# Moving the row maxima of attention to the steps with products with v, and two start times in the layer behind it

## The chip, the cores and the metric

The kernel is one program on one core of a Trainium2 chip. A core has a matrix engine (PE, with its weight loads shown apart as PEld), a vector engine (DVE), a scalar engine (ACT), GpSimd (POOL), and SyncE (SP), whose queue issues most DMAs. Each engine works through its own instructions in the order in which they were written, and waits on semaphores where it needs what another engine makes. The metric is the device time of one execution in microseconds; the median of the runs is compared.

## The reference

The work is attention over 32 heads (4 batches of 8) with pooled queries, then a dense layer with a gate, then a mixture of experts. The part that the change touches is the first, and the start of the second:

```python
q_pool = q.reshape(B, H, S // 2, 2, D).mean(axis=3)
scores = scale * np.matmul(q_pool, k.transpose(0, 1, 3, 2))
scores = scores - np.max(scores, axis=-1, keepdims=True)
attn = np.exp(scores)
attn = attn / (np.sum(attn, axis=-1, keepdims=True) + 1e-09)
x = np.matmul(attn, v)                      # 576 queries, 1152 keys, 64 columns a head
...
h = x @ w_in                                # 2304 tokens, 512 -> 2048
x = (h * (1.0 / (1.0 + np.exp(-1.702 * h)))) @ w_out
```

## The kernel before

**Attention** works on 16 pairs of heads, one after the other; a pair's two heads stand on partitions 0 to 63 and 64 to 127. A pair is 14 steps, one for each entry of UNITS: steps 0 to 8 take 320 queries against one block of 128 keys, steps 9 to 12 take the other 256 queries against two blocks, step 13 against the last one. The loop counter `g` runs over all steps of all pairs, and `p, i = divmod(g, NU)` with NU = 14.

At each step `score_unit` has PE compute the scores (tile `ss`, eight or sixteen matmuls in pairs, one of a pair for each head): products of the high and low parts of q and k, and one product of ONE with M, which subtracts the row's maximum. ACT then takes the exponential (tile `E`). Two steps behind, `av_group` multiplies groups of E by v (tile `av`), always at steps 4, 7, 10, 13 and 1 (AV_AT). GpSimd adds E up for the row sums (`acc`, `ds`), except for the first three blocks, which DVE reduces (`r`, at steps 4 and 10). `den` turns the sums into `dn` on PE at step 10 of the next pair.

**The maxima** come ahead of the scores, since M must be there at a pair's step 0. `max_unit(p, i)` is one of 14 units for a pair: units 0 to 11 are two matmuls (tile `xs`, 384 keys, one for each head), unit 12 is two and unit 13 one with a block-diagonal operand `BD` that holds the last queries of both heads. Behind each matmul DVE reduces the tile to a maximum (L233). The tiles come from a pool of three PSUM buffers, which the transposed maxima (`mt`) use too. Behind unit 13 `max_rows` reduces to `m9`, and two steps later `max_rows_put` has PE transpose it (`mt`), DVE split it in `mh` and `ml`, and SP bring both to M by eight small DMAs. Before the change each step has one unit, LEAD = 19 steps ahead of the score step with the same number, so a pair's last unit stands at step 8 of the pair before it.

The order within a step is: score, unit, rows, products with v, den, what the agenda `ag` holds for this step (r, mt, pieces of the weights' conversion, x), GpSimd's sums, then BESIDE, which prepares coming pairs (loads, `q_high`, `k_high`, at step 7 `q_low` on DVE and `k_low` on GpSimd). Agenda entries for the weights and x stand at steps 13 and 1.

**The dense layer** (`ffn`) goes through chunks of tokens, the first of 768 in two pieces. A step is twelve matmuls of layer 1 into `h` (two PSUM buffers), a gate on ACT and DVE, and two steps later nine matmuls of layer 2 into `acc`. In the first chunk the weights still arrive as 8-byte floats, and each of 28 blocks is converted by seven DVE instructions (L453 to L459) and three on ACT (L461 to L463). `blocks` is a generator that gives them one by one, and `fill(n)` writes the next n of them into the queues: three and then three or four at each step of the first chunk. ACT's share is written by `act` at the following step. For the next chunk `xload` brings a tile of x and the reciprocals of its row sums into `xraw`, of which there is one buffer; `xnorm` multiplies them, for chunk 1 on DVE; `xsplit` makes high and low parts.

Of the kernel before, what the change touches and what calls it, by code (L numbers as in the profile page):

```python
# [39 lines left out]
def pieces(n):  # L40
    k = -(-n // 384)
    return [(i * (n // k), n // k) for i in range(k)]
# [6 lines left out]
NU = len(UNITS)  # L49
EARLY = 2  # L50
AV_AT = (4, 7, 10, 13, 1)
GROUPS = [range(0, 3), range(3, 6), range(6, 9), range(9, 12), range(12, 14)]


# [17 lines left out]
class Kernel:  # L72
# [54 lines left out]
    def attention(self, ctx):  # L127
# [11 lines left out]
        N = NPAIR  # L139
# [23 lines left out]
        ag = Agenda()  # L163
# [71 lines left out]
        def max_rows(p):  # L235

            m9 = sm.tile([P, 9], F32, name="m9", tag="m9")
            V.reduce_max(m9, st[p]["mx"], axis=AX.X)
            max_rows_put(0, m9) if p == 0 else ag.at(ag.now + 2, max_rows_put, p, m9)
# [90 lines left out]
            for u in range(2):  # L330
                eng.dma_start(self.DEN[hp * 2 + u:hp * 2 + u + 1, b * Q:b * Q + Q], dr[64 * u:64 * u + 1])

        LEAD = 19

        BESIDE = [(0, v_load, 1), (2, q_high, 2), (3, k_high, 2, 0), (4, k_high, 2, 1), (5, k_high, 2, 2),
                  (7, q_low, 1), (7, k_low, 1), (8, loads, 3), (13, q_add, 3)]
# [21 lines left out]
        for u in range(2):  # L358
            g = NU * 1 + 3 + u * (NU * 3 + 6)
            calm = [x for x in range(g + 7, g + 5 * NU) if x % NU in AV_AT[3:]]  # L360
            ag.at(g, self.wload, u)
            ag.at(g + 6, weights, u, [g + 6, *calm[:6], calm[4] + 1, calm[5] + 1, calm[6]])

        for u in range(2, 2 * EARLY):
            g = NU * (N - 1) - 5 + 8 * (u - 2)
# [3 lines left out]
            ag.at(NU * N - 8 + 5 * n, self.wload, 2 * EARLY + n)  # L369
        for b in range(8):  # L370
            ag.at(NU * (8 + b) + AV_AT[3] - 10, operands, b % 4, b // 4)
        for g in range(-LEAD, NU * N + 20):
            p, i = divmod(g, NU)
            ag.now = g
            if 0 <= p < N:
                score_unit(p, i)
            px, ix = divmod(g + LEAD, NU)
            if 0 <= px < N:
                max_unit(px, ix)
                if ix == NU - 1:  # L380
                    max_rows(px)
            pa, ia = divmod(g - 2, NU)
            for j, r in enumerate(GROUPS):
                if 0 <= pa < N and ia == r[-1]:
                    av_group(pa, j)
            if i == 10 and 0 < p <= N:
                den(p - 1)
            ag.run(g)
            if 0 <= p < N:
                sum_unit(p, i)  # L390
            for f, *of in start.get(g + LEAD, ()):
                f(*of)
            for step, f, ahead, *of in BESIDE:
                if step == i and 0 <= p and p + ahead < N:
                    f(p + ahead, *of)
            if g == -LEAD + 12:
                empty_lists()
            if i == 12 and 1 <= p < N and p % 4 == 0:
                self.recip(sm, p // 4 - 1, ag, 9)
            if g == NU * N:  # L400
                nc.scalar.activation(warm[:, 1:2], warm[:, 0:1], AF.Sigmoid)
# [89 lines left out]
    def ffn(self, ctx):  # L491
# [34 lines left out]
        ag = Agenda()  # L526
# [38 lines left out]
        def fill(k):  # L565
            for _ in range(k):
                f = fq.pop(0) if fq else next(splits, None)
                if f:
                    f()
# [181 lines left out]
                fq.append(fin)  # L751

        constants()
        steps = [(c, fb, pc) for c in range(len(CH)) for fb in range(NF) for pc in range(len(pieces(CH[c])))]
        first = {(c, fb): g for g, (c, fb, pc) in reversed(list(enumerate(steps)))}
        LAG = 2
        for g in range(len(steps) + LAG):
            ag.now = g
            if g < len(steps):
                c, fb, pc = steps[g]  # L760
                fa, fb_ = (2, 3) if CH[c] >= 384 else (1, 2)
                if g == 2:
                    self.recip(sm, B - 1, ag, 3)
                if c == 0:
                    fa, fb_ = 3, 3 + pc
                layer1(c, fb, pc, fa, fb_)
                if fb == 0 and pc == 0 and c + 1 < len(CH):
                    for j in range(ND):
                        for q in range(len(pieces(CH[c + 1]))):
                            g0 = first[0, 12] + 2 * j - 1 if c == 0 else first[c, 4] + 2 * j  # L770
                            ag.at(g0, xload, c + 1, j, q)
                            ag.at(g0 + 1, xnorm, c + 1, j, q)
                            ag.at(first[c, NF - 1] if c == 0 else g0 + 4, xsplit, c + 1, j, q)
            if g >= LAG:
                c2, f2, p2 = steps[g - LAG]
                layer2(c2, f2, p2)
                if f2 == NF - 1:
                    if c2 == 0 and p2 == 0:
                        while splits.gi_frame:
                            fill(1)  # L780
                            act()
                        rctx.close()
                        late["o"] = self.pool(ctx, "m_o", 2)
                        late["wg"] = late["o"].tile([P, 9, DM], F32, name="wg", tag="wg", bufs=1)
                        dma(late["wg"][:, 0:8], self.wgT.partition_broadcast(P))
                        dma(late["wg"][:, 8], self.w_skip.partition_broadcast(P))
                        for d in range(ND):
                            dma(wgd[:, d, 0:8], self.wgT[:, d * P:d * P + P].rearrange("e p -> p e"))
                            dma(wgd[:, d, 8:9], self.w_skip[d * P:d * P + P].rearrange("(p a) -> p a", a=1))
                    o, n = pieces(CH[c2])[p2]  # L790
                    grp = tuple((C0[c2] + o) // P + i for i in range(n // P))
                    if c2 < len(CH) - 1:
                        todo.extend((grp, i) for i in range(len(grp)))
            if g < len(steps) + LAG - 1:
                rstep()
                ag.run(g)
            if not (self.first or todo or fq or live[0]) and self.listed == NT - CH[-1] // P:

                self.first = late["o"].tile([P, 9, DM], F32, name="first", tag="wg", bufs=1)
                for m in range(4):  # L800
                    self.first_expert_load(m)
                for m in range(8):
                    ag.at(max(g + 2 + m // 2, first[len(CH) - 1, m] + LAG + 1), self.first_expert_split, m)

                ps = hp.tile([P, 8], F32, name="cn", tag="h")
                nc.tensor.matmul(ps, ONE, mac[self.listed], start=True, stop=True)
                V.tensor_scalar(self.early, ps[:, 0:1], P - 0.5, float(P), op0=ALU.is_gt, op1=ALU.mult)
                dma(self.ids_e, self.LIST[0:P])
                V.memset(self.x_e, 0.0)
                nc.gpsimd.indirect_dma_start(  # L810
                    out=self.x_e, out_offset=None, in_=self.X2[0:C0[-1]],
                    in_offset=bass.IndirectOffsetOnAxis(ap=self.ids_e[:, 0:1].bitcast(U32), axis=0),
                    bounds_check=C0[-1] - 1, oob_is_err=False,
                )
# [270 lines left out]
```

## Time and profile before

| | |
|---|---|
| median of 3 runs | 1052.24 us (1047.6 to 1054.67) |
| the profiled execution, its own time | 1049.92 us |
| its span | 1048.1 us |
| PE busy | 996.8 us, 95% |
| DVE busy | 768.9 us, 73% |
| ACT busy | 501.9 us, 48% |
| POOL busy | 454.2 us, 43% |
| mean granted clock of TensorE | 0.984 |

The span is from the first to the last instruction; 1.8 us of the execution lie around it. Matmuls are pipelined, so PE counts as busy while the next matmul is held back by less than the last one's tail; what a group of matmuls costs is read from the start of its first to the start of what follows it. A timeline row gives the start, the length of the merged instructions, engine, line, operation, the tiles written and read, the shapes and the count, and in brackets the idle time before it with what ended it.

### The profile page before, as it was taken

How to read it: one execution, taken by the hardware profiler on the slowest of the kernel's cores; microseconds unless marked ns; L12 is line 12 of the kernel's file. 1: busy time of each engine (PE TensorE's matmuls, PEld its weight loads, DVE VectorE, ACT ScalarE, POOL GpSimd, SP SyncE). 2: the span in 40 equal slices, each digit the busy share in tenths (PEclk: the TensorE clock that was granted, in tenths of full speed). 3: DMA queues.
4: the chain of work that ended last, by engine and by line, in shares of the span. 5: the costliest groups of instructions: out<-in, count | busy, mean ns of one | idle time of the engine just before them, and what ended most of it. 6: DMA issues, size and time to landing. Idle time of an engine off the chain costs nothing. (4 is left out here: it accounts for less than half of the span.)

```text
span 1048.1 us, 18986 instructions
## 1 busy us (share of the span) xinstructions
PE 996.8 (95%) x7002; PEld 787.3 (75%) x7002; DVE 768.9 (73%) x1643; ACT 501.9 (48%) x928; POOL 454.2 (43%) x306
## 2 busy tenths in 40 slices
PE   6999999999999999999997999999999997998994
PEld 4766667666766676698886888888889885876773
DVE  7767777778877778799977689787575564656824
ACT  2555555555555554655644422332333261555723
POOL 3798999999999998500000001101111003223212
PEclk9999999999999999999999999999999998998998
DMA  4232232223333322333342520212211234738501
GB/s 166 67 101 81 81 101 82 81 81 97 97 96 96 97 72 71 99 102 122 123 132 81 173 71 16 71 33 60 71 48 44 81 115 145 266 105 285 164 21 51
DMA packets 64321, 103.34 MB, mean 99 GB/s; under 512 B 18630, under 2 KB 34630, under 8 KB 64072
## 3 DMA queue, kind: packets, MB, share of 16 engines
q1 hardware_dynamic: 60068, 96.34, 28.6%
q0 software_dynamic: 3904, 5.15, 1.6%
q8 instruction: 67, 1.10, 0.4%
q14 instruction: 54, 0.44, 0.1%
q10 hardware_dynamic: 228, 0.30, 0.1%
HBM read 90.04 MB, written 17.35 MB: 102 GB/s over the span
## 5 line engine op out<-in xcount | busy, mean ns | idle before, releaser
L233 DVE TENSOR_REDUCE mx<-xs 128x1 f32<-128x384 f32 x432 | 212.7, 550 | 75.5 <-PE xs L230 70.1
L274 ACT ACTIVATE E<-ss 128x640 f32<-128x640 f32 (+1 forms) x224 | 174.0, 787 | 149.0 <-PE ss L273 120.7
L290 POOL TENSOR_TENSOR acc<-acc,E 128x640 f32<-128x640 f32 (+1 forms) x94 | 179.4, 1909 | 16.4 <-ACT E L274 12.3
L310 PE MATMUL av<-E,v 128*64 128x256 f32 (+1 forms) x1152 | 157.1, 413 | 0.0
L599 PE MATMUL h<-xh,wih 128*128 128x384 f32 (+1 forms) x448 | 141.3, 315 | 9.9 <-ACT wih L463 7.7
L599 PE MATMUL h<-xh,wil 128*128 128x384 f32 (+1 forms) x448 | 140.0, 312 | 0.6 <-DVE wil L459 0.5
L599 PE MATMUL h<-xl,wih 128*128 128x384 f32 (+1 forms) x448 | 139.9, 312 | 0.1
L476 POOL TENSOR_TENSOR xa<-xraw 128x256 f32<-128x256 f32 (+1 forms) x16 | 15.5, 970 | 261.3 <-DMA xraw<-RD 256.1
L310 PEld LDWEIGHTS av<-E,v 128*64 128x64 f32 x1152 | 75.6, 136 | 56.0 <-issue 15.0
L626 PE MATMUL acc<-woh,gl 128*128 128x512 f32 x288 | 114.8, 399 | 0.0
L624 PE MATMUL acc<-woh,gh 128*128 128x512 f32 x288 | 114.8, 399 | 0.0
L625 PE MATMUL acc<-wol,gh 128*128 128x512 f32 x288 | 114.5, 398 | 0.0
L230 PE MATMUL xs<-kh,qh 64*128 64x384 f32 x384 | 101.9, 388 | 7.9 <-ACT kh L210 7.2
L273 PE MATMUL ss<-qh,kh 64*128 64x320 f32 (+1 forms) x576 | 107.3, 339 | 2.0 <-ACT E L274 2.0
L604 ACT ACTIVATE g<-h 128x384 f32<-128x384 f32 (+1 forms) x112 | 49.4, 441 | 116.1 <-PE h L599 116.0
L606 ACT ACTIVATE gh<-g 128x384 fp32r<-128x384 f32 (+1 forms) x112 | 53.8, 480 | 104.6 <-DVE g L605 104.6
L599 PEld LDWEIGHTS h<-xh,wih 128*128 128x128 f32 x448 | 84.2, 188 | 18.5 <-ACT wih L463 11.0
L643 DVE CUSTOM_DVE_ANT_0 junk<-xs,wg 128x512 bf16<-128x512 f32 x135 | 95.5, 707 | 2.0
L605 DVE TENSOR_TENSOR g<-h,g 128x384 f32<-128x384 f32 (+1 forms) x112 | 55.7, 497 | 55.9 <-ACT g L604 54.5
L273 PE MATMUL ss<-M,ONE 64*128 64x320 f32 (+1 forms) x576 | 94.2, 294 | 0.7 <-DMA M<-ml 0.6
L273 PE MATMUL ss<-qh,kl 64*128 64x320 f32 (+1 forms) x576 | 92.2, 293 | 0.0
L273 PE MATMUL ss<-ql,kh 64*128 64x320 f32 (+1 forms) x576 | 92.1, 293 | 0.0
(195 smaller groups left out, 2069.6 us busy)
## 6 DMA issues: line engine op xcount, KB each, us to landing
stage<-w SPq DMA_DIRECT2D x40, 512.0 KB
qd<-qT SPq DMA_DIRECT2D x16, 576.0 KB
v<-v SPq DMA_DIRECT2D x16, 576.0 KB
kr<-kT SPq DMA_DIRECT2D x15, 576.0 KB
wr<-w_in SPq DMA_DIRECT2D x16, 512.0 KB
wr<-w_out SPq DMA_DIRECT2D x16, 512.0 KB
X<-xs SPq DMA_DIRECT2D x18, 256.0 KB
out<-xs SPq DMA_DIRECT2D x18, 256.0 KB
```

The costliest lines, as they stand in the source:

```text
L230: nc.tensor.matmul(ps[:, :384], q, k[:, part * 384:part * 384 + 384], start=True, stop=True)
L233: V.reduce_max(o, ps[:, :384], axis=AX.X)
L273: nc.tensor.matmul(ps[:, u, j * w:j * w + w], k[HALF[u]], q[HALF[u], qs], start=(n == 0), stop=(n == 3))
L274: nc.scalar.activation(place(p, i), ps[:, :, :len(kbs) * w], AF.Exp, scale=0.5 / D ** 0.5)
L290: G.tensor_tensor(d["a"], d["a"], place(p, i), op=ALU.add)
L310: nc.tensor.matmul(d["av"][HALF[u], :w], d["v"][:, u, kb], e[:, u, n * w:n * w + w], start=(kb == 0), stop=(kb == KB - 1))
L599: nc.tensor.matmul(h, a[:, d * P:d * P + P], x, start=(k == 0), stop=(k == 3 * ND - 1))
L605: V.tensor_tensor(g, h, g, op=ALU.mult)
L624: nc.tensor.matmul(acc[t], gh[:, ts], bh, start=(fb == 0), stop=False)
L625: nc.tensor.matmul(acc[t], gh[:, ts], bl, start=False, stop=False)
L626: nc.tensor.matmul(acc[t], gl[:, ts], bh, start=False, stop=(fb == NF - 1))
L643: V.tensor_tensor_reduce(out=junk, in0=R[grp[i]], in1=late["wg"][:, e], op0=ALU.mult, op1=ALU.add, scale=1.0, scalar=0.0, accum_out=R[grp] ...
```

## The change

The maxima are no longer written one unit a step. An iterator over all units hands out the next one where it is asked for: at steps 1, 3, 4, 6, 7, 9, 10, 12 and 13 in the place where the unit stood before, and at steps 1, 4, 7, 10 and 13, those with products with v, a second time behind everything else of the step. Steps 0, 2, 5, 8 and 11 have none. Twenty units, no longer nineteen, stand ahead of the first score step, so that at the start of a pair units 0 to 5 of the next one are done; its unit 12 comes at step 7, unit 13 behind q's low part at step 7, and the transpose at step 9.

In the dense layer eight pieces of the conversion are written ahead of the first step, and for chunk 1 the loads of x stand two steps earlier and the multiplications one step earlier.

```diff
 AV_AT = (4, 7, 10, 13, 1)
+MAX_AT = (*AV_AT, 3, 6, 9, 12)
...
-        LEAD = 19
+        LEAD = 20
...
+        units = iter([(p, i) for p in range(N) for i in range(NU)])
+
+        def maxima():
+            for p, i in units:
+                max_unit(p, i)
+                if i == NU - 1:
+                    max_rows(p)
+                break
+
         for g in range(-LEAD, NU * N + 20):
             p, i = divmod(g, NU)
             ag.now = g
             if 0 <= p < N:
                 score_unit(p, i)
-            px, ix = divmod(g + LEAD, NU)
-            if 0 <= px < N:
-                max_unit(px, ix)
-                if ix == NU - 1:
-                    max_rows(px)
+            if g < 0 or i in MAX_AT:
+                maxima()
...
             for step, f, ahead, *of in BESIDE:
                 if step == i and 0 <= p and p + ahead < N:
                     f(p + ahead, *of)
+            if g >= 0 and i in AV_AT:
+                maxima()
...
         constants()
+        fill(8)
         steps = [(c, fb, pc) for c in range(len(CH)) for fb in range(NF) for pc in range(len(pieces(CH[c])))]
...
-                            g0 = first[0, 12] + 2 * j - 1 if c == 0 else first[c, 4] + 2 * j
+                            g0 = first[0, 12] + 2 * j - 3 if c == 0 else first[c, 4] + 2 * j
                             ag.at(g0, xload, c + 1, j, q)
-                            ag.at(g0 + 1, xnorm, c + 1, j, q)
+                            ag.at(g0 + 2 if c == 0 else g0 + 1, xnorm, c + 1, j, q)
```

On PE, from the products with v of step 13 to those of step 1 (`ss` are the scores, `xs` the maxima, `av` the products with v), this stands before:

```order
L310 MATMUL av<-E,v 64x256 x12
L273 MATMUL ss<-qh,kh 128x320 x2
L273 MATMUL ss<-qh,kl 128x320 x2
L273 MATMUL ss<-ql,kh 128x320 x2
L273 MATMUL ss<-M_1_128,ONE 128x320 x2
L230 MATMUL xs<-kh,qh 128x384 x2
L273 MATMUL ss<-qh,kh 128x320 x2
L273 MATMUL ss<-qh,kl 128x320 x2
L273 MATMUL ss<-ql,kh 128x320 x2
L273 MATMUL ss<-M_1_128,ONE 128x320 x2
L230 MATMUL xs<-kh,qh 128x384 x2
L310 MATMUL av<-E,v 64x256 x6
```

And this stands there now:

```order
L311 MATMUL av<-E,v 64x256 x12
L231 MATMUL xs<-kh,qh 128x384 x2
L274 MATMUL ss<-qh,kh 128x320 x2
L274 MATMUL ss<-qh,kl 128x320 x2
L274 MATMUL ss<-ql,kh 128x320 x2
L274 MATMUL ss<-M_1_128,ONE 128x320 x2
L274 MATMUL ss<-qh,kh 128x320 x2
L274 MATMUL ss<-qh,kl 128x320 x2
L274 MATMUL ss<-ql,kh 128x320 x2
L274 MATMUL ss<-M_1_128,ONE 128x320 x2
L231 MATMUL xs<-kh,qh 128x384 x2
L311 MATMUL av<-E,v 64x256 x6
```

The unit that stood between two score steps now stands directly behind the long products with v of step 13, and two score steps follow each other.

On DVE, from step 4 to step 10 (`mx` are the maxima of a tile, `r` a row sum, `ql` q's low part, `m_...` is m9, `mh` and `ml` the split of the transposed maxima), this stands before:

```order
L69 TENSOR_REDUCE r<-E 128x320
L233 TENSOR_REDUCE mx<-xs 128x1 x6
L203 TENSOR_TENSOR ql<-qd,qh 128x576
L233 TENSOR_REDUCE mx<-xs 128x1
L238 TENSOR_REDUCE m_1577<-mx 128x9
L233 TENSOR_REDUCE mx<-xs 128x1 x4
L69 TENSOR_REDUCE r<-E 128x320
L246 TENSOR_SCALAR mh<-mt 9x128
L247 SCALAR_TENSOR_TENSOR ml<-mt,mh 9x128
```

And now:

```order
L70 TENSOR_REDUCE r<-E 128x320
L234 TENSOR_REDUCE mx<-xs 128x1 x6
L204 TENSOR_TENSOR ql<-qd,qh 128x576
L234 TENSOR_REDUCE mx<-xs 128x1
L239 TENSOR_REDUCE m_1567<-mx 128x9
L234 TENSOR_REDUCE mx<-xs 128x1 x2
L247 TENSOR_SCALAR mh<-mt 9x128
L248 SCALAR_TENSOR_TENSOR ml<-mt,mh 9x128
L234 TENSOR_REDUCE mx<-xs 128x1 x2
L70 TENSOR_REDUCE r<-E 128x320
```

DVE's own order hardly moves: what moves is where PE hands over the tiles between these rows, and mh and ml, which come a unit and a row sum earlier.

On DVE at the start of the dense layer (`mac` is the last of attention's and the constants' work, `g` and `gl` belong to the gate, the rows on `wr` and `t` are pieces of the conversion), this stands before:

```order
L523 MEMSET mac_6160 128x4
L605 TENSOR_TENSOR g<-h,g 128x384
L453 TENSOR_SCALAR t_6214<-wr 128x512
L454 TENSOR_SCALAR t_6215<-t_6215 128x512
L455 SCALAR_TENSOR_TENSOR t_6214<-wr,t_6214 128x512
L609 TENSOR_TENSOR gl<-g,gh 128x384
```

And now:

```order
L532 MEMSET mac_6160 128x4
L462 TENSOR_SCALAR t_6195<-wr 128x512
L463 TENSOR_SCALAR t_6196<-t_6196 128x512
L464 SCALAR_TENSOR_TENSOR t_6195<-wr,t_6195 128x512
L465 TENSOR_SCALAR t_6196<-t_6196 128x512
L466 SCALAR_TENSOR_TENSOR t_6196<-wr,t_6196 128x512
L462 TENSOR_SCALAR t_6205<-wr 128x512
L467 TENSOR_SCALAR sg<-t_6196 128x512
L463 TENSOR_SCALAR t_6206<-t_6206 128x512
L614 TENSOR_TENSOR g<-h,g 128x384
```

Eight pieces now stand ahead of the first gate, the second and the last of which read what ACT makes of the weights.

## Rows read from the trace of the kernel before

**Rows 1.** Windows: stretch, length, busy PE, PEld, DVE, ACT, POOL, clock, DMA, GB/s.

```profile
213.07:239.03 25.96, 25.96 (x253) 18.15 (x252) 20.18 (x37) 14.93 (x25) 23.77 (x14) 1.00 0.27 80
...
442.67:518.23 75.56, 75.56 (x383) 68.32 (x382) 70.64 (x156) 43.82 (x87) 0.00 (x0) 1.00 0.35 116
518.23:580.80 62.57, 53.94 (x253) 46.00 (x252) 49.01 (x106) 30.51 (x59) 0.00 (x0) 0.97 0.33 101
```

**Rows 2.** Waits of the whole run: total us, times, longest.

```profile
PEld xs L230 <- DVE mx L233: 20.8, 109, 0.8
```

**Rows 3.** Timeline of PE, steps 0 to 11 of one pair.

```profile
207.31 0.33 PE L230 MATMUL xs<-kh,qh 64*128 64x384 f32 x2
207.48 0.31 PE L273 MATMUL ss<-qh,kh 64*128 64x320 f32 x2
...
208.07 0.66 PE L230 MATMUL xs<-kh,qh 64*128 64x384 f32 x2
208.66 1.51 PE L310 MATMUL av<-E,v 128*64 128x256 f32 x12
...
211.55 0.66 PE L230 MATMUL xs<-kh,qh 64*128 64x384 f32 x2
...
213.07 1.84 PE L310 MATMUL av<-E,v 128*64 128x320 f32 x12
...
216.27 0.67 PE L230 MATMUL xs<-kh,qh 64*128 64x384 f32 x2
...
217.45 0.62 PE L230 MATMUL xs<-kh,BD 128*128 128x384 f32 x2
218.00 1.84 PE L310 MATMUL av<-E,v 128*64 128x320 f32 x12
...
220.54 0.45 PE L230 MATMUL xs<-kh,BD 128*128 128x384 f32 x1
220.92 0.39 PE L273 MATMUL ss<-qh,kh 64*128 64x256 f32 x2
...
223.10 0.34 PE L230 MATMUL xs<-kh,qh 64*128 64x384 f32 x2
223.37 1.84 PE L310 MATMUL av<-E,v 128*64 128x320 f32 x12
...
226.10 0.28 PE L243 MATMUL mt<-ident,m 128*9 128x128 f32 x1
226.31 0.39 PE L273 MATMUL ss<-qh,kh 64*128 64x256 f32 x2
```

**Rows 4.** Timeline of all engines, DVE's rows in the same pair.

```profile
201.77 3.08 DVE L233 TENSOR_REDUCE mx<-xs 128x1 f32<-128x384 f32 x6 [0.73 <-PE xs L230]
```

**Rows 5.** Timeline of PE at the start.

```profile
21.25 4.81 PE L230 MATMUL xs<-kh,qh 64*128 64x384 f32 x10
```

**Rows 6.** Timeline of PE: first matmul of steps of the dense layer.

```profile
451.12 0.34 PE L599 MATMUL h<-xh,wih 128*128 128x384 f32 x1
...
518.23 0.34 PE L599 MATMUL h<-xh,wih 128*128 128x384 f32 x1
...
552.96 0.45 PE L599 MATMUL h<-xh,wih 128*128 128x384 f32 x1 [3.72 <-ACT wih L463]
...
580.80 0.34 PE L599 MATMUL h<-xh,wih 128*128 128x384 f32 x1
```

**Rows 7.** Timeline of DVE in the dense layer.

```profile
445.57 0.56 DVE L605 TENSOR_TENSOR g<-h,g 128x384 f32<-128x384 f32 x1 [3.58 <-ACT g L604]
...
550.28 0.56 DVE L476 TENSOR_TENSOR xa<-xraw 128x384 f32<-128x384 f32 x1 [2.34 <-DMA xraw<-RD]
...
563.38 0.56 DVE L476 TENSOR_TENSOR xa<-xraw 128x384 f32<-128x384 f32 x1 [2.82 <-DMA xraw<-RD]
```

**Rows 8.** Timeline of SP's queue: the first load of x for chunk 1.

```profile
541.49 1.56 SPq L83 DMA_DIRECT2D xraw<-X  x1
```

**Rows 9.** Line 203, q's low part: ns min, median, max, first and last start.

```profile
L203 DVE TENSOR_TENSOR ql<-qd,qh x15: 1484/1498/1884, 37.3 to 402.2; 128x576 fp32r<-128x576 f32 x15
```

## The prediction, made before the changed kernel was run

> **What bounds the kernel now.** I began with the busy shares: PE 95%, and the next engine, DVE, 73%. A busy PE is no proof that it is at its best, so I looked for places where it takes longer than the same work takes elsewhere. There are two: the maxima in attention, and the last third of the first chunk of the dense layer.
>
> In attention one pair of heads takes 25.96 us [rows 1]. PE has something in flight all the time, GpSimd is busy for 23.77 us, DVE for 20.18 and ACT for 14.93. The list of waits shows PE's weight loads for maxima held back by DVE 109 times, 20.8 us in all [rows 2]. The timeline of one pair shows what that costs. A unit of maxima is two matmuls, one for each half of the array, which run side by side: 0.17 us from their start to that of the scores behind them (207.31 to 207.48), and 0.27 with products with v behind them (223.10 to 223.37), so a change from half to full rows costs 0.10. But at step 1 the same unit takes 0.59 us (208.07 to 208.66) [rows 3]. DVE needs 3.08 us for six tiles, 0.51 each [rows 4], and three buffers hold the tiles. The second tile of a unit takes the buffer of the first tile of the unit before, one score step earlier. Two units in successive short steps therefore hold PE: its second matmul comes late and then runs alone.
>
> In the dense layer an undisturbed step takes 4.19 us ((518.23 - 451.12) / 16 steps). From 518.23 to 580.80 stand twelve steps, which should take 50.3 us and take 62.57 [rows 6]: 12.2 us are lost, with PE waiting for converted weights, 3.72 us of it at 552.96. DVE is the source: twice it stands at the multiplication of x until its load has landed, 2.34 and 2.82 us, and the conversion queues behind that [rows 7].
>
> **The change, maxima.** I go through the segments between products with v, and write only what differs. The segment from step 13 to 1 has a unit between scores now and one in front of the products. The first goes behind the products of step 13, where PE changes its rows anyway; that pair costs 0.17 + 0.10 and the scores behind it no longer pay the change: nothing gained or lost. The second has two score steps and no unit ahead of it, so it takes 0.27 in place of 0.59: minus 0.32. From step 1 to 4: step 2's unit moves likewise; steps 3 and 4 keep theirs. From 211.55 to 213.07 they take 1.52 us [rows 3]; with step 3 undisturbed and step 4 still hindered this is 0.17, 0.59 for the scores (207.48 to 208.07) and 0.59: 1.35: minus 0.17. From step 4 to 7: step 5's unit moves, 6 and 7 stay; 216.27 to 218.00 is 1.73 us, and becomes 0.17 + 0.59 + 0.55, the last from 217.45 to 218.00 [rows 3], for which I grant nothing: minus 0.42. From step 7 to 10: the single block-diagonal tile, 0.38 us between scores (220.54 to 220.92) with two row changes around it that others pay, goes directly behind the products, where I put it at 0.28: minus 0.30. But the transpose `mt`, 0.21 us behind dn (226.10 to 226.31), now stands between maxima and scores and brings its two changes along: plus 0.41. Together plus 0.11. From step 10 to 13: the transpose is gone, minus 0.21; the unit of step 11 moves behind dn; steps 12 and 13 hinder each other as before.
>
> The sum is 0.32 + 0.17 + 0.42 - 0.11 + 0.21 = 1.01 us a pair, of 25.96. Pairs 0 to 13 have all of it (units end at step 7 of pair 14): 14.1 us.
>
> Against it stand two terms. The twentieth unit ahead of the first score lies in a phase that DVE sets: ten tiles take 4.81 us there [rows 5], so two more cost 0.96, say 1.0 (bounds 0.3, two unhindered tiles, and 2.0, if the load of M that runs beside them is late as well). And DVE has a piece of weights or x at step 1 that now stands ahead of the second unit; where this is long, step 3 waits for that unit's buffer. Some six pairs have one of the long pieces; at 0.2 each, the mean wait of rows 2, this is 1.0 (0 to 3). Maxima: minus 14.1 + 1.0 + 1.0 = minus 12.1. The bounds: if the three units that I left hindered go free too, each gains up to 0.32 more, 14 pairs x 0.96 = 13 us further; if the waits come back in full at other places, the gain is 0 and the two terms stay, plus 2.
>
> The moved reductions cost DVE nothing new: the same 27 tiles a pair. At 24.95 us a pair DVE's 20.18 would be 81%, GpSimd's 23.77 would be 95%. The next late thing is thus GpSimd, not DVE.
>
> **The change, dense layer.** Eight pieces of the conversion go into time in which DVE idles: 3.58 us before the first gate [rows 7]. At DVE's mean of 0.45 us an instruction in this layer (70.64 / 156, [rows 1]) they are 3.6 us, but the second and the eighth also need ACT, which still handles attention's last rows. I expect the first gate about 1.5 to 2 us late; the third step of layer 1 needs its PSUM buffer, and holds PE for about 1.0 us (0 to 2). In return every later block is ready 8 / 6.5 = 1.2 steps, 5.2 us, earlier, more than any single wait of PE in that stretch. The two loads: the first x was issued at 541.49 [rows 8] and multiplied at 550.28 [rows 7], 8.8 us later. Before, one step of 4.19 us and DVE's lag lay between issue and use, now two steps, 8.4. The first load, which waits for no buffer, is in time; each of the others is issued behind the multiplication before it and may be some 0.5 us late, which the 5.2 us of lead cover. I put 1.0 us for what is left. Dense layer: minus 12.2 + 1.0 + 1.0 = minus 10.2 (minus 12.2 if nothing is left; minus 4.8 if two loads still hold PE for 3.7 us each, as at 552.96).
>
> **The sum.** 1049.92 - 12.1 - 10.2 = 1027.6 us against the profiled execution. The median of the runs shown is 2.3 us above that execution and the three spread over 7 us, so I say 1028.
>
> **Rivals.** *GpSimd takes the gain of attention.* It has 23.77 us of work a pair and idles 2.19 [rows 1]; if that idle time is bound to its order (each first addition waits for a new E), pairs stay at 25.96 and only the dense layer gains: 1049.92 + 2 - 10.2, about 1042. Against it: the sums are needed only at step 10 of the next pair, so GpSimd can lag behind for several microseconds and idle less. The Trainium skill bears on this ("SBUF — State Buffer", Who interferes with whom): a DVE reduction never contends with GpSimd for the port that they share, while a DVE instruction with two inputs in SBUF does. By that the moved reductions would not lengthen GpSimd's additions, and this rival would lose its best reason; no row here separates the two. I give it 0.10.
>
> *The transpose waits for m9: slower than before.* PE works in order, and `mt` now stands at step 9, behind unit 13, which on DVE is queued behind q's low part of 1.50 us [rows 9]. Counted from PE's start on unit 12: the first tile is there after 0.45 (the row of 220.54), DVE ends both at about 1.5, q's low part at 3.0, unit 13 at 3.5, and m9, which I put at no more than a tile, by 4.0. PE reaches mt after 0.55 for unit 12, 2.54 for the products of step 7 and the scores of step 8 (218.00 to 220.54), 0.28 for unit 13 and 1.09 for scores and unit of step 9 (half of 220.92 to 223.10) [rows 3]: 4.46. There is 0.46 us of room. If DVE comes to step 7 late, or q's low part is drawn out, PE stands still at every pair with all scores behind it. From 0.46 + 22.3 / 14 = 2.05 us of lateness on all gain is gone, and at 3.2 us the kernel needs 14 x 1.15 = 16 us more than before: 1066. Against it: q's low part never took more than 1.88 us in 15 cases [rows 9], 0.38 over its median. The same section of the skill says that of DVE and GpSimd the one that comes second waits for the other's whole instruction; the spread in rows 9 shows less than that. 0.04.
>
> *The loads stay late.* If the load takes as long as now, 8.8 us, and its issue still follows the multiplication of the one before, DVE waits 2 to 3 us at three of four tiles, and the lead of 5.2 us is used up by the second: 1049.92 - 12.1 - 4.8, about 1033. 0.14.
>
> *Waits go altogether.* 1049.92 - 12.1 - 13 - 11.2, about 1014. 0.06.
>
> **How the numbers follow.** The forecast, from 1020 to 1032, has 0.60; the rest, with 0.06 for smaller gains in both parts (about 1038), is above. The range of 8 in 10 reaches up to GpSimd's rival and down almost to the last: 1015 to 1042. A measurement of this kernel tells about 1% (10.5 us) from no change. Faster by over 1% means below 1041.7: the forecast, the late loads, the lucky case, the smaller gains and a third of GpSimd's rival, 0.88, of which I take 0.03 off for what I have not seen: 0.85. Slower 0.05, the rest 0.10.
>
> **What would show it.** Pairs of about 25.0 us between the first products with v of one and the next, the segment from 4 to 7 at 4.5 us (now 4.93) and from 13 to 1 at 4.46 (now 4.78); the unit at step 1 at 0.27; that at steps 4 and 13 still near 0.6; no wait of PE at mt. In the dense layer no wait of DVE at xraw above 1 us and fewer than 3 us lost where 12.2 were. I am wrong if pairs stay near 26 with GpSimd idling less than 1 us, if PE waits at mt, or if the waits for weights are still there.

## The result, and the profile after

The changed kernel takes 1037.3 us (median of 4 runs, 1035.77 to 1040.74), the kernel before 1053.24 beside it. The ratio is 0.9863, with a 95% interval from 0.9827 to 0.9898; ratios here are formed from all runs of both kernels and not from the two medians, which lie 15.9 us apart. A second set of runs gave 0.9858 (0.9832 to 0.9884). The forecast was 1028, with a range from 1015 to 1042. Sign and range held, but the gain is 14.4 us by the ratio where 22.3 were summed up.

The profiled execution took 1035.77 us, against 1049.92 of that before. The head of its page, busy time of each engine:

```profile
span 1034.1 us, 18977 instructions
...
PE 987.3 (95%) x7002; PEld 780.6 (75%) x7002; DVE 775.4 (75%) x1643; ACT 499.9 (48%) x928; POOL 456.8 (44%) x306
```

Shares tell little, so I split the 14.0 us between the two spans at events that both traces have. The last product with v ends 2.13 us earlier (441.22 before, 439.09 after). From there to the first `h` it takes 0.70 longer, since PE's last `dn` waits 1.00 us for DVE, which is at the last row sums, where it waited 0.33. The first 33 steps of the dense layer (32 of the first chunk, one of the next) take 135.96 us where they took 146.51: minus 10.55. What follows is 2.08 shorter, which lies inside the spread of executions: in the repeat of the changed kernel it is 3.23 longer than here. The dense layer thus gave its 10 us; attention gave 2 of 12, and 0.70 of these go again before the first `h`.

The windows of the changed kernel answer to [rows 1]: first one pair of heads, then steps 0 to 16 and 17 to 30 of the dense layer.

```profile
211.24:236.73 25.49, 25.42 (x252) 17.71 (x252) 19.57 (x35) 14.84 (x25) 23.87 (x14) 1.00 0.27 83
441.24:509.87 68.63, 67.33 (x342) 60.80 (x340) 65.15 (x144) 40.83 (x81) 0.00 (x0) 1.00 0.37 120
509.87:568.50 58.63, 58.63 (x296) 52.79 (x295) 53.87 (x117) 33.13 (x65) 0.00 (x0) 1.00 0.41 120
```

A pair takes 25.49 us, not 24.95. GpSimd idles 1.62 of them, 2.19 before [rows 1]. In the last window 14 steps take 58.63, which is 4.19 each: nothing is lost there, where 12.2 us were.

PE's timeline of a pair answers to [rows 3]; it begins with the unit of step 1, and the first product with v below is that of step 1, the others those of steps 4, 7 and 10.

```profile
207.71 0.34 PE L231 MATMUL xs<-kh,qh 64*128 64x384 f32 x2
207.97 1.52 PE L311 MATMUL av<-E,v 128*64 128x256 f32 x12
...
210.87 0.34 PE L231 MATMUL xs<-kh,qh 64*128 64x384 f32 x2
...
211.93 0.36 PE L231 MATMUL xs<-kh,qh 64*128 64x384 f32 x2
212.22 1.84 PE L311 MATMUL av<-E,v 128*64 128x320 f32 x12
213.99 0.44 PE L231 MATMUL xs<-kh,qh 64*128 64x384 f32 x2
...
215.44 0.34 PE L231 MATMUL xs<-kh,qh 64*128 64x384 f32 x2
...
216.59 0.62 PE L231 MATMUL xs<-kh,BD 128*128 128x384 f32 x2
217.14 1.84 PE L311 MATMUL av<-E,v 128*64 128x320 f32 x12
218.91 0.44 PE L231 MATMUL xs<-kh,BD 128*128 128x384 f32 x1
...
221.18 0.28 PE L244 MATMUL mt<-ident,m 128*9 128x128 f32 x1
...
222.73 1.83 PE L311 MATMUL av<-E,v 128*64 128x320 f32 x12
```

The unit of step 1 takes 0.26 us (207.71 to 207.97) where it took 0.59, as forecast. That of step 4 is free as well, 0.29 (211.93 to 212.22), which was not; that of step 13 takes 0.44 us, 0.62 before. From step 4 to 7 (212.22 to 217.14) it is 4.92 us, as before: nothing was gained. From the row of 215.44 on I measure 1.70 us to the product, where 1.73 stood [rows 3] and 1.31 was forecast.

The timeline of all engines shows who holds PE in that stretch (`ss` is the scores, `E` their exponentials):

```profile
215.06 0.70 ACT L275 ACTIVATE E<-ss 128x640 f32<-128x640 f32 x1 [0.60 <-PE ss L274]
...
215.82 0.19 PEld L274 LDWEIGHTS ss<-qh,kh 64*128 64x128 f32 x2 [0.33 <-ACT E L275]
...
216.59 0.30 PEld L231 LDWEIGHTS xs<-kh,BD 128*128 128x128 f32 x2 [0.19 <-DVE mx L234]
```

Steps 5 and 6 now have their scores back to back, since step 5's unit has gone. The scores at 215.82 are those of step 7. They need the buffer of step 5, whose exponential ends at 215.76, so the unit in front of them pays 0.38 in place of 0.17. The scores themselves take 0.77 (215.82 to 216.59), where the forecast has 0.59. The block-diagonal pair takes 0.55 as before: two matmuls with full rows, 0.28 from one start to the next. It does not wait for DVE. The 0.19 in front of it, which the view puts down to `mx`, is there as `issue` in a kernel in which ACT's part is halved (a row in the experiments). Over pairs (60 to 390 us) the waits read:

```profile
PEld xs L231 <- DVE mx L234: 11.0, 35, 0.9
...
PEld ss L274 <- ACT E L275: 9.4, 32, 0.3
...
PEld mt L244 <- DVE m L239: 3.3, 3, 1.1
PE mt L244 <- DVE m L239: 2.5, 3, 0.8
```

In the same stretch of the kernel before, weight loads of maxima waited for DVE 75 times (13.9 us in all), those of scores for ACT 10 times (4.9 us). So the waits for DVE are fewer by half, and waits for ACT have come. The first line still says too much of DVE: 13 of its 35 entries are the 0.19 us at the block-diagonal pair, and 11 are idle times of 0.38 to 0.39 us behind the products of step 1, as long as those behind step 13's, which end in `issue`. Some 11 are left. In the kernel before, only the 13 at the block-diagonal pair can be told to be of this kind. The last two lines are new: three times PE stands at the transpose. One of these places, first PE, then DVE ahead of it:

```profile
169.96 0.28 PE L244 MATMUL mt<-ident,m 128*9 128x128 f32 x1 [0.83 <-DVE m L239]
```

```profile
165.89 1.10 DVE L420 TENSOR_SCALAR rt<-rt 128x36 f32<-128x36 f32 x1
167.03 0.38 DVE L421 RECIPROCAL rt<-rt 128x36 f32<-128x36 f32 x1
167.32 1.90 DVE L204 TENSOR_TENSOR ql<-qd,qh 128x576 fp32r<-128x576 f32 x1
169.14 0.55 DVE L234 TENSOR_REDUCE mx<-xs 128x1 f32<-128x384 f32 x1
169.72 0.18 DVE L239 TENSOR_REDUCE m<-mx 128x9 f32<-128x27 f32 x1
```

Once in four pairs DVE makes reciprocals of row sums at step 7. They stand ahead of q's low part, and the row maxima `m` come 0.83 us too late for PE. (q's low part is longer too: 1.69 us in the median, where [rows 9] have 1.50.) The segment from 7 to 10 is 6.47 us there, 5.59 in the other pairs.

The sums by segments over pairs 0 to 13, after minus before, set against the forecast (14 times the number of a pair):

| from one product with v to the next | forecast, us | measured, us |
|---|---|---|
| start, to the first product with v | +1.0 | +1.89 |
| 13 to 1 | -4.5 | -4.95 |
| 1 to 4, with DVE's pieces at step 1 | -2.4 + 1.0 | +0.22 |
| 4 to 7 | -5.9 | -0.28 |
| 7 to 10 | +1.5 | +5.05 |
| 10 to 13 | -2.9 | -2.67 |
| pair 14 | not counted | -1.4 |
| sum | -12.1 | -2.1 |

In the dense layer the cost stands on PE, the third step's wait for its buffer (first line), and DVE's multiplications of x answer to [rows 7]:

```profile
446.96 0.44 PE L608 MATMUL h<-xh,wih 128*128 128x384 f32 x1 [1.30 <-DVE g L614]
```

```profile
544.00 0.56 DVE L485 TENSOR_TENSOR xa<-xraw 128x384 f32<-128x384 f32 x1 [2.04 <-DMA xraw<-RD]
...
552.31 0.55 DVE L485 TENSOR_TENSOR xa<-xraw 128x384 f32<-128x384 f32 x1
```

Loads still hold DVE, here for 2.04 us and 4.1 in all, but PE, which has converted weights in store, loses almost nothing by it: one step, the first of chunk 1, is 0.32 us longer.

### The profile page after: what moved, and what is told of

It is laid out like the page before. It is cut to its first block, busy times and chain, and to the rows that moved or that the text cites. A ratio compares the mean times of both kernels' runs of the same rounds, so it can differ in the third digit from the quotient of the medians.

```text
span 1034.1 us, 18977 instructions
## 1 busy us (share of the span) xinstructions
PE 987.3 (95%) x7002; PEld 780.6 (75%) x7002; DVE 775.4 (75%) x1643; ACT 499.9 (48%) x928; POOL 456.8 (44%) x306
## 5 line engine op out<-in xcount | busy, mean ns | idle before, releaser
L234 DVE TENSOR_REDUCE mx<-xs 128x1 f32<-128x384 f32 x432 | 217.0, 551 | 80.4 <-PE xs L231 79.2
L274 PE MATMUL ss<-qh,kh 64*128 64x320 f32 (+1 forms) x576 | 97.3, 325 | 2.3 <-ACT E L275 1.5
L231 PE MATMUL xs<-kh,qh 64*128 64x384 f32 x384 | 90.3, 408 | 9.5 <-ACT kh L211 7.1
L608 PEld LDWEIGHTS h<-xl,wih 128*128 128x128 f32 x448 | 84.2, 188 | 5.2 <-DVE xl L498 0.7
L274 PE MATMUL ss<-qh,kl 64*128 64x320 f32 (+1 forms) x576 | 88.0, 294 | 0.0
L274 PE MATMUL ss<-ql,kh 64*128 64x320 f32 (+1 forms) x576 | 87.9, 294 | 0.0
```

The source lines that it names most:

```text
L231: nc.tensor.matmul(ps[:, :384], q, k[:, part * 384:part * 384 + 384], start=True, stop=True)
L234: V.reduce_max(o, ps[:, :384], axis=AX.X)
L274: nc.tensor.matmul(ps[:, u, j * w:j * w + w], k[HALF[u]], q[HALF[u], qs], start=(n == 0), stop=(n == 3))
L608: nc.tensor.matmul(h, a[:, d * P:d * P + P], x, start=(k == 0), stop=(k == 3 * ND - 1))
```

## The experiments

**The parts alone.** Two kernels are the kernel before with the dense layer's part, and with the maxima's part; two more have one half of the dense part each. The dense part:

```diff
+        fill(8)
-  g0 = first[0, 12] + 2 * j - 1 if c == 0 else first[c, 4] + 2 * j
+  g0 = first[0, 12] + 2 * j - 3 if c == 0 else first[c, 4] + 2 * j
-  ag.at(g0 + 1, xnorm, c + 1, j, q)
+  ag.at(g0 + 2 if c == 0 else g0 + 1, xnorm, c + 1, j, q)
```

> The kernel before with the two edits of the dense layer alone. If the two parts of the change add up as their traces say, this one gives nearly all of the gain: the dense layer's first chunk took 10.9 us less in the trace of the changed kernel, so 11 us less than before (ratio 0.9895). The rival, that the dense layer only profits because attention left its engines in another state, gives less than 6 us.

> The changed kernel without its two edits of the dense layer: the moved maxima alone. From the traces attention ends 1.4 to 2.1 us earlier: 1 to 3 us less than before (ratio 0.997 to 0.999). My prediction had 12 us less (0.9885); if this run shows that, the loss lies in how the two parts meet and not in the maxima.

> The kernel before with the eight early pieces alone. If the lead of 5.2 us is what counts, the short waits for weights (some 2 us in all) go and the two long ones, behind DVE's waits of 2.3 and 2.8 us for x, shrink: 6 to 9 us less. If the waits for x are the cause by themselves, 2 to 3 us less and PE's wait of 3.7 us stays.

> The kernel before with the earlier loads of x alone. If the waits for x are the cause by themselves, DVE no longer waits for them and 7 to 9 us go; the short waits for weights before them (0.4 to 0.7 us at every second step) stay. If the lead is what counts, waits of 2 us and more for weights stay near the end of the chunk, and 3 to 5 us go.

| kernel | median, us | ratio to before | interval | first 33 steps, us (146.51 before) |
|---|---|---|---|---|
| dense part alone | 1042.83 | 0.9913 | 0.9893 to 0.9933 | 136.01 |
| maxima alone | 1048.79 | 0.9953 | 0.9931 to 0.9975 | 147.96 |
| pieces ahead of the layer alone | 1051.31 | 0.9979 | 0.9967 to 0.9991 | 144.57 |
| loads alone | 1043.76 | 0.9912 | 0.9886 to 0.9938 | 139.84 |

The parts add up: 0.87% and 0.47% are 1.34%, and both together give 1.37%. Maxima alone repeat the segments of the changed kernel to 0.06 us (-4.94, +0.20, -0.27, +5.07, -2.71), so nothing of attention's shortfall comes from the dense part. By time, maxima are worth 5.0 us (2.6 to 7.3, from the interval), more than the 1 to 3 that were expected. Of the dense part, the loads are what counts. With the pieces alone DVE still stands at late loads, as its rows below show. PE loses 1.88 and 1.76 us in steps 28 and 29, where the lead is used up, and 5.13 in step 32, the first of chunk 1, which waits for x itself:

```profile
551.92 0.56 DVE L476 TENSOR_TENSOR xa<-xraw 128x384 f32<-128x384 f32 x1 [3.11 <-DMA xraw<-RD]
...
563.91 0.56 DVE L476 TENSOR_TENSOR xa<-xraw 128x384 f32<-128x384 f32 x1 [2.99 <-DMA xraw<-RD]
```

With the loads alone no wait of DVE at x is left, and PE has only short ones, the two lines below of its list from 441 to 580 us.

```profile
PEld h L599 <- ACT wih L463: 5.8, 7, 1.3
PE h L599 <- ACT wih L463: 2.6, 4, 0.8
```

The eight pieces save a further 3.8 us of the first 33 steps in the trace; the times, 0.9913 and 0.9912, don't confirm them, with intervals of 2 to 3 us either way.

**Who holds the segment from 4 to 7: ACT or DVE?** Three versions of the changed kernel. The first reduces half of each maxima tile (its maxima are of half the keys, the time of the reduction falls). The second makes exponentials of one of two heads at steps 2, 5 and 11, with ones for the other; tokens then go to other experts, so only its attention pairs are read. The third does both. (The whole times of the last two, 1070.03 and 1049.04 us, therefore say nothing here.)

```diff
-  V.reduce_max(o, ps[:, :384], axis=AX.X)
+  V.reduce_max(o, ps[:, :192], axis=AX.X)
```

```diff
-  nc.scalar.activation(place(p, i), ps[:, :, :len(kbs) * w], AF.Exp, scale=0.5 / D ** 0.5)
+  n = 1 if p and i in (2, 5, 11) else 2
+  if n == 1:
+      V.memset(place(p, i)[:, 1], 1.0)
+  nc.scalar.activation(place(p, i)[:, :n], ps[:, :n, :len(kbs) * w], AF.Exp, scale=0.5 / D ** 0.5)
```

> The changed kernel with each maximum taken over the first half of a tile's 384 keys. It subtracts a number that may be smaller than the row's maximum; the division by the row sum takes that out again. A reduction lasts some 0.3 us in place of 0.51. Theory A: scores of steps 4, 7 and 13 wait for the exponential two steps before them, and this sets the pair; then the pair stays near 25.3 us (25.5 in the changed kernel), the segment from 4 to 7 above 4.75. Theory B: DVE's reductions still hold PE through the three buffers; then the pair falls to 24.7 us or less and the segment from 4 to 7 to 4.5.

> The changed kernel with the exponentials of steps 2, 5 and 11 taken for one head alone from the second pair on, the other half of the tile being set to one on DVE; the experts get other tokens by it, so only the pairs of attention are read. ACT's instruction is half as long there. Theory A: scores at 4, 7 and 13 no longer wait; segment from 4 to 7 from 4.92 to 4.6, from 10 to 13 from 6.29 to 6.05, the pair near 24.9 us unless the maxima then hold PE. Theory B: the pair stays near 25.5 us.

> Both at once: maxima over half a tile and, at steps 2, 5 and 11, the exponentials of one head. Theory A and B together, each holding PE where the other is taken away: the pair falls to 24.3 us, segment from 4 to 7 to 4.45, while each alone gives less than half of it. If a third thing sets the pair, GpSimd with its 23.8 us for one, it stays above 24.9.

Segments of a steady pair, in us:

| from, to | after | half the reduction | half the exponentials | both |
|---|---|---|---|---|
| 4 to 7 | 4.92 | 4.92 | 4.66 | 4.65 |
| 7 to 10 | 5.59 | 5.58 | 5.59 | 5.58 |
| 10 to 13 | 6.29 | 6.10 | 6.28 | 6.09 |
| 13 to 1 | 4.46 | 4.46 | 4.46 | 4.46 |
| 1 to 4 | 4.25 | 4.23 | 4.25 | 4.05 |

Each theory is right in one place. From 4 to 7 ACT decides: a faster DVE changes nothing there. From 10 to 13 DVE does. From 1 to 4 only both together make PE faster. A pair takes 25.29 us with half the reduction, as theory A has it, 25.24 with half the exponentials, between the two theories, and 24.83 with both, where 24.3 were expected. The column of the exponentials holds for the undisturbed pairs 3, 4 and 7 alone. That kernel gives DVE three instructions of 0.33 us more in each pair (they write the ones), and in the other ten of pairs 1 to 13 the segment from 1 to 4 takes 4.37 to 5.01 us, so that attention ends no earlier (439.32 us, 439.09 in the changed kernel). What a faster ACT alone would do from 1 to 4 and from 10 to 13, without these instructions, is not shown. Half the exponentials at step 5, one row of ACT, one of the weight loads and four of PE:

```profile
214.74 0.44 ACT L278 ACTIVATE E<-ss 128x320 f32<-128x320 f32 x1 [1.63 <-PE ss L274]
```

```profile
216.01 0.30 PEld L231 LDWEIGHTS xs<-kh,BD 128*128 128x128 f32 x2 [0.19 <-issue]
```

```profile
215.13 0.34 PE L231 MATMUL xs<-kh,qh 64*128 64x384 f32 x2
215.30 0.34 PE L274 MATMUL ss<-qh,kh 64*128 64x320 f32 x2
...
216.01 0.62 PE L231 MATMUL xs<-kh,BD 128*128 128x384 f32 x2
216.56 1.84 PE L314 MATMUL av<-E,v 128*64 128x320 f32 x12
```

The unit of step 6 now costs 0.17 (215.13 to 215.30), as forecast for the changed kernel; from it to the product it is 1.43 us. The forecast's 1.31 isn't reached, since step 7's scores take 0.71 (215.30 to 216.01) where 0.59 was taken: 0.59 was read in front of a half-row unit, and here full rows follow. The block-diagonal pair takes the 0.55 of the forecast, with the reductions halved too. With the reductions halved, pairs 9 to 12 also lose their long segment from 1 to 4 (4.22 to 4.24, where it is 4.74 to 4.77), and the first product with v comes at 29.26 us, not 33.35. The whole kernel took 1023.96 us in its one run, the kernel before 1053.49 beside it. In the trace attention ends 9.9 us earlier than in the changed kernel, 4.1 of them at the start: so much hangs on the length of DVE's reductions.

**The transpose, and x's low part.** Two waits of the changed kernel could be moved away by a number each. A repeat of the changed kernel stood beside them.

> The changed kernel as it is, on the same chip as the three behind it: 14 us less than before (ratio 0.9863 as first measured). What it shows besides is whether the clock rises as late at the start as in the first trace (31.8 us against 28.9 before): with the change that is a cause, otherwise chance.

```diff
-  ... else ag.at(ag.now + 2, max_rows_put, p, m9)
+  ... else ag.at(ag.now + 3, max_rows_put, p, m9)
```

> The changed kernel with the transpose of the maxima one step later, at step 10 behind dn, where it stood before the change. Theory: at step 9 it costs two changes between half and full rows a pair and, in the three pairs in which DVE also takes reciprocals ahead of q's low part, a wait for m9 of 0.8 us. Then the segment from 7 to 10 falls from 5.59 to 5.2 and that from 10 to 13 rises from 6.29 to 6.5: 0.2 us a pair or 3 us, and 2.6 us from the three pairs: 4 to 6 us less than the changed kernel. Rival: nothing but the place moves and less than 1.5 us are gained.

The repeat first, on the start. Scores' matmuls last 0.47 us each up to 31.5 us in the first trace of the changed kernel, and 0.31 soon after. In the repeat they do so up to 29.8, with the maxima alone up to 28.7, in the kernel before up to 28.3, and with the dense part alone, whose attention is that of the kernel before, up to 29.4. The granted clock reads 1.00 in all these stretches. The place thus moves from one execution to the next, and a part of the first trace's late start is chance: the first product with v comes 1.89 us later there, 1.35 in the repeat, 1.19 with the maxima alone.

With the transpose one step later the time is 1037.07, 0.9849 (0.982 to 0.9878), the repeat's 1038.41, 0.9858: no difference that can be told. In the trace the segment from 7 to 10 falls to 5.18 in most pairs and to 5.78 in the three with reciprocals, and 10 to 13 rises to 6.49: 0.21 a pair net. But in pairs 1, 8, 12, 13 and 14 segments grow by 0.14 to 1.1 (pair 14 from 1 to 4: 5.97, 4.87 in the changed kernel). The last product ends at 437.08, 1.6 us before that of the repeat (438.64). The expected 4 to 6 us weren't there.

x's low part stands on DVE ahead of the second unit of step 1 in pairs 9 to 12, and is long beside GpSimd. Two rows of the changed kernel, and the same operation when attention's sums on GpSimd are over:

```profile
287.48 1.91 DVE L498 TENSOR_TENSOR xl<-xraw,xh 128x384 fp32r<-128x384 f32 x1
289.31 1.94 DVE L234 TENSOR_REDUCE mx<-xs 128x1 f32<-128x384 f32 x4
...
438.67 0.55 DVE L498 TENSOR_TENSOR xl<-xraw,xh 128x384 fp32r<-128x384 f32 x1
```

Issued one step later, at step 2, on top of the transpose's move:

```diff
-  ag.at(ag.now + 12, self.xlow, raw[:, 0], 0, j, pc)
+  ag.at(ag.now + 13, self.xlow, raw[:, 0], 0, j, pc)
```

> As the one before, and the low part of x one step later, at step 2, behind the second unit of step 1. In pairs 9 to 12 that piece takes 1.9 us on DVE ahead of the second unit and the segment from 1 to 4 takes 4.77 in place of 4.25 us. Theory: that segment returns to 4.25 in all pairs, 2 us less. Rival: the piece then stands in the way of the unit of step 3 and nothing is gained.

It gained nothing: 1040.76, 0.9885 (0.9858 to 0.9912). The segment from 1 to 4 rises from 4.77 to 5.07, since the piece now stands ahead of the unit of step 3. DVE's rows of this kernel:

```profile
287.27 1.31 DVE L498 TENSOR_TENSOR xl<-xraw,xh 128x384 fp32r<-128x384 f32 x1
288.51 1.94 DVE L234 TENSOR_REDUCE mx<-xs 128x1 f32<-128x384 f32 x4
```

Next, the same kernel with the old start (19 units ahead of the first score, the twentieth at step 0):

```diff
-        LEAD = 20
+        LEAD = 19
-            if g < 0 or i in MAX_AT:
+            if g <= 0 or i in MAX_AT:
```

> As the one before, with nineteen units ahead of the first score and the twentieth at the first pair's step 0. Theory: DVE sets the pace there, 0.5 us a tile, so the first score comes 0.8 us earlier again and the first products with v at 31.5 to 32.5 us in place of 33.35: 1 to 2 us less than the one before, and the fastest of all, 6 to 9 us below the changed kernel. Rival: the clock's rise sets the start, and the first products with v stay where they were.

The first product with v comes at 32.00 where it came at 33.01, the expected microsecond; the time, 1040.09, 0.9874 (0.9846 to 0.9902), can't tell 1 us. It isn't the fastest of all, as was expected; the repeat of the changed kernel has 0.9858.

**Earlier in place of later.** The last kernel moves all three pieces of x ahead, and keeps the moves of transpose and start:

```diff
-  ag.at(ag.now + 10, self.xnorm, raw[:, 0], raw, 0, j, pc, V)
-  ag.at(ag.now + 11, self.xhigh, raw[:, 0], 0, j, pc)
-  ag.at(ag.now + 12, self.xlow, raw[:, 0], 0, j, pc)
+  ag.at(ag.now + 7, self.xnorm, raw[:, 0], raw, 0, j, pc, V)
+  ag.at(ag.now + 8, self.xhigh, raw[:, 0], 0, j, pc)
+  ag.at(ag.now + 10, self.xlow, raw[:, 0], 0, j, pc)
```

> The changed kernel with the transpose at step 10, nineteen units ahead of the first score (the twentieth at the first pair's step 0), and the three pieces of x at steps 10, 11 and 13 in place of 13, 0 and 1, so that DVE has its two while PE is on dn and on the long products with v, and none ahead of the second unit of step 1. Theory: the segment from 1 to 4 is 4.25 in pairs 9 to 12 (4.77 in the changed kernel, 5.07 with the low part at step 2), the first products with v start near 32.0; 3 to 5 us less than the changed kernel, near 1034. Rival: at step 10 the piece delays the second unit, the segments from 10 to 13 grow by 0.3 or more in pairs 8 to 14, and the time stays at 1037 or above.

It is the fastest of the kernels that leave no work out: 1033.4 us (1031.98 to 1037.86, 6 runs), 0.9803 (0.9773 to 0.9833), near the 1034 that were expected. The changed kernel's repeat has 0.9858 (0.9832 to 0.9884); the two intervals just touch. Against the kernel in which only the transpose moved (0.9849, 0.982 to 0.9878) they overlap, so what x alone brings is read from the traces. DVE's rows in the same part of it:

```profile
279.68 0.96 DVE L498 TENSOR_TENSOR xl<-xraw,xh 128x384 fp32r<-128x384 f32 x1
282.01 1.02 DVE L234 TENSOR_REDUCE mx<-xs 128x1 f32<-128x384 f32 x2 [1.37 <-PE xs L231]
```

The piece now ends well ahead of the maxima, at a place where DVE waits for PE anyway. Pairs 9 to 12 take 4.25 us from 1 to 4, pair 14 takes 3.88 in place of 4.87, and the last product with v ends at 432.57, 6.5 us earlier than in the changed kernel. Of these, 3.8 stand between steps 7 and 13, where the transpose moved, 1.4 at the start, 2.3 from 1 to 4 and 0.6 in pair 14; 1.5 are lost from 13 to 1. Moving x costs something as well: in pair 8 its low part takes 2.73 us (at 253.72), and the segment from 13 to 1 takes 6.04 us where it took 5.54.

## Why the prediction was right in sign and range, and 9 us off in size

**Dense layer: right.** Minus 10.2 was forecast; the trace has minus 10.55, the times of this part alone minus 9.2 (7 to 11). Its cost was 1.45 us at the first steps (the 1.30 us at 446.96 among them), forecast 1.0 with bounds of 0 and 2; what is left of the losses is 0.3, forecast 1.0, so these two errors nearly cancel. What was misjudged is which half does it: I wrote that the lead of 5.2 us would cover late loads. By the runs the earlier loads alone give all of the gain that can be timed, and the lead without them 2.2 us (0.9979).

**Maxima: the term was mis-sized**, minus 12.1 where the times show minus 5.0 and the trace minus 2.1. Step by step:

- *13 to 1, and 10 to 13: right*, 4.46 and 6.29 us; 4.46 and 6.26 were forecast (6.47 before, minus 0.21).
- *4 to 7: this step failed.* The sentence was "becomes 0.17 + 0.59 + 0.55". I let the first term follow from DVE alone. The unit that was taken out of step 5 had kept the scores apart, and with two score steps in succession ACT's exponential, 0.70 us, is the late one. Halving the exponentials frees 0.26 us of this segment, halving the reductions none: 3.6 us of the 5.6 that the sum lacks here. Most of the rest is the second term, 0.59, where scores in front of full rows take 0.71: 1.7 us. The third, 0.55, was right, but the bounds counted it among three units that could go free, and two full-row matmuls can't: it stays 0.55 with both halved.
- *7 to 10: mis-sized by 3.5 us.* The block-diagonal tile behind the products costs 0.37 (218.91 to 219.28), not 0.28, and `mt` waits in three of the pairs, 0.88 us each (these pairs were 0.2 longer than the others before the change too). The rival that ends slower described that wait, with 0.46 us of room. By my own sign ("if PE waits at mt") I was wrong in these three. In other pairs the room was there: PE does not stand at mt. But its only source for DVE's queue was q's low part; I had not looked for what DVE does only in every fourth pair. The same room, once broken, costs 2.6 us and not the 16 that would have made the kernel slower.
- *1 to 4: minus 0.16 a pair, as forecast (0.17), by two errors that cancel.* Step 3's unit to the product takes 1.35 us (210.87 to 212.22), as I had it, but not as 0.17 + 0.59 + 0.59: the last unit is free, and the scores of step 4 begin late. Only with both halvings does this segment shrink, to 4.05. And the pieces at step 1 cost about 2.5 us (0.52 in each of four pairs, 0.23 in two), where 1.0 stood, inside its bounds of 0 to 3. "The mean wait of rows 2" was the wrong row: the duration of the piece itself was to be had, up to 1.57 us in the trace of the kernel before (1.91 in that of the changed one).
- *Start:* plus 1.89 in this profile, 1.35 in the repeat, where 1.0 stood (0.3 to 2.0).

**The rivals.** GpSimd does not take the gain: it idles 1.62 us in a pair of 25.49, and in the kernel with both halvings pairs shrink to 24.83 us. Next in line was ACT, which at 14.84 us of 25.49 looked the freest of all. The loads' rival half came true (DVE waits 4.1 us for loads, in two places), almost without cost. The time landed on the case of "smaller gains in both parts (about 1038)", which had 0.06; but only one part had a smaller gain. (The chances named for a gain of over 1% add up to 0.89, not 0.88.)

The Trainium skill ("SBUF — State Buffer", Who interferes with whom) was cited for the reductions, which it says never contend with GpSimd, while a DVE instruction with two inputs in SBUF does. Both agree with these traces: a reduction of 384 columns lasts 0.54 to 0.56 us in each of the 432 cases of the changed kernel, 330 of them with GpSimd at work throughout and 29 with GpSimd idle, while x's low part takes 0.55 us alone and up to 1.91 beside GpSimd.

**What stays open:** why the times give maxima 5.0 us where the trace gives 2 to 3 (with maxima alone the end of attention is 2.85 us earlier, the first `h` 2.16); one profiled execution against a median with an interval from 2.6 to 7.3 can't settle it. The trace of the kernel before is of a quick execution, 1049.92 us, where 17 runs have a median of 1053.81. And whether the eight pieces ahead of the dense layer gain anything beside the earlier loads. A third buffer for scores, which would try the finding on ACT without leaving work out, was not tried.

## What to carry to other kernels

When a unit of work is taken out between two others that share a double buffer, price the consumer of that buffer too: here the exponential of 0.70 us, on an engine busy for 58% of a pair, took back nearly all that DVE's relief could give in that segment. Price a group also by what stands behind it: the same scores cost 0.59 us in front of half rows and 0.71 in front of full ones. A piece that queues ahead of the critical work is priced by its own duration at that hour, and by its rarest neighbours: DVE's work of every fourth pair decided whether PE waited. And look for a place where the queue idles before looking for a later one: x's low part one step later lengthened its segment, and the three pieces of x moved ahead, with two other moves, were in the kernel that came out fastest.

## What the runs showed of the hardware that was not expected

The same subtraction of 128x384 values on DVE took 0.55 us when GpSimd was idle, and 0.96, 1.31 and 1.91 us at three places beside its additions (rows above). Beside them it was also 0.55 once (392.43 us in the changed kernel, GpSimd at work throughout) and 2.73 (in the last kernel): no fixed factor, and no run here took apart what sets it. A reduction from PSUM kept to 0.54 to 0.56 us in the same pairs. And a change between half and full rows on PE again showed as about 0.10 us at each place: 0.26 to 0.29 for a unit in front of products, 0.17 in front of scores.
